# Output stores moved to ScalarE's queue, constants and copies spread over three engines: a fused attention and mixture-of-experts kernel on Trainium2

## The chip, the cores and the metric

The kernel runs on one core of one Trainium2 chip. In it TensorE does the matrix products, VectorE, ScalarE and GpSimd the elementwise work, and SyncE issues transfers, as do GpSimd and, after the change, ScalarE. The granted clock is the share of TensorE's full clock that the trace shows. The metric is the device time of one launch in microseconds (us), the median of several runs; the outputs are compared with the reference each time. A run is labelled slow when it is more than 1.5 per cent above the fastest of its kernel; ratios use the other runs only.

## The reference, cut to what matters

Eight batches, eight heads, 576 tokens, 64 values a head. Each batch goes through attention with a window of 32 tokens to either side, then the whole batch goes to one of eight experts, chosen by the mean of its attention output.

```python
scores = scale * np.matmul(q, k.transpose(0, 1, 3, 2))     # |i - j| <= 32 only
attn = np.exp(scores); attn = attn / attn.sum(-1)
x = attn @ v                                               # (8, 576, 512)
logits = x.mean(axis=1) @ w_gate                           # pick one expert e per batch
out[b] = gate * (np.maximum(x[b] @ w1[e], 0.0) @ w2[e])    # w1 512x1024, w2 1024x512
```

The expert isn't known before the batch's attention is done, so its 4 MB of weights are asked for at that moment, from an address read out of a register.

## The kernel before

A small planner in the kernel's Python holds a list of operations, each with an engine, an estimated duration, what it depends on and which buffers it takes and frees. It simulates them and emits a fixed order for each engine. What it believes of a transfer therefore decides the order in which instructions stand. The parts that matter here (cuts are marked `# ...`):

```python
buffers("osb", [P, DM], FP32, 3)          # output tiles of 128 tokens, three of them
# ...
end = at[op.eng] = t + op.dur
over = end + self.LAT[op.eng]
if op.land:                               # transfers: one after another at 370 GB/s
    dma_at = max(dma_at, end + 1.3) + op.land / (self.DMA_GBS * 1e3)
    over = dma_at + 0.7                   # from here on the planner takes it as landed
# ...
def loadw(op):                            # expert weights, fp32 to fp16, by GpSimd's DMA queue
    nc.gpsimd.dma_start(w1s, moe_w1[ds(ereg, 1)][0].rearrange("(p dt) f -> p dt f", p=P))
# ...                                     # loadw2 the same for w2
def evac(op, i=i):                        # ScalarE: PSUM -> osb, times the gate
    osb = op.got["osb"][0]
    nc.scalar.activation(osb[:, 0:w], bank_of.pop(f"2{b}{i}")[:, 0:w], ACTF.Copy, ...)
plan.add("ACT", 0.69 if i < 4 else 0.43, f"V{b}{i}", evac, ..., takes=[("osb", 1)])

def store(op, i=i):                       # SyncE: osb -> DRAM, five tiles a batch
    if i < 4:
        nc.sync.dma_start(out[b, 128 * i : 128 * i + 128, :], osb); return
    for c in range(2):
        nc.sync.dma_start(out[b, 512:576, 256 * c : 256 * c + 256], osb[64 * c : 64 * c + 64, 0:256])
plan.add("SP", 0.6 if i < 4 else 1.2, f"O{b}{i}", store, deps=[f"V{b}{i}"], frees=[(f"V{b}{i}", "osb")], ...)
```

An eviction is ScalarE's copy of a finished result out of PSUM, the memory that TensorE writes. A batch has five evictions (four of 128 tokens and a tail of 64) and three `osb` tiles. The fourth eviction needs the tile of the first, so it needs the first store landed; the fifth needs the second.

The softmax here doesn't subtract the row's maximum and nothing guards it: scores larger than these inputs give would overflow.

## Time and profile before

| | before |
|---|---|
| median of 3 runs | 276.94 us (276.49 to 279.07) |
| span of the profiled run | 277.2 us |
| TensorE busy | 227.2 us |
| mean period from batch to batch (six of them) | 28.6 us |
| landing of a store, median of 33 away from weights / of 15 beside them | 2.2 / 10.5 us (5.7 to 17.2) |

TensorE is the busiest engine, and it still stands or runs at half clock for long enough that the run is much longer than its work. From the page of the kernel before: the first line of the busy times, and the shares of the chain of work that ended last (followed back from the last instruction).

```profile
PE 227.2 (82%) x2432; PEld 174.5 (63%) x2432; DVE 160.0 (58%) x447; ACT 155.2 (56%) x329; POOL 72.3 (26%) x86
...
PE 53%; DVE 21%; DMA 14%; ACT 6%; issue 4%; POOLq 0%; ACTq 0%; DVEq 0%; SPq 0%
```

### The profile page before, as it was taken

The page shows a single profiled execution, that of the slowest core. Times are in us where ns is not written, and L with a number is a line of the kernel's source. Part 1 is how long each engine was busy: PE and PEld are TensorE (multiplying, and loading weights), DVE is VectorE, ACT ScalarE, POOL GpSimd, SP SyncE. Part 2 cuts the span into 40 slices and gives each one's busy share as a digit, 9 for nine tenths or more (in the row PEclk, how much of TensorE's full clock was granted, in tenths as well). Part 3 has the DMA queues.
Part 4 walks back from the last instruction along what each step waited for, and adds up shares of the span by engine and source line. Part 5 has one row for each costly group of instructions (what it writes and reads, how often), then busy time and mean ns, then how long its engine had stood idle before and what let it go on. Part 6 is the DMA issues. An engine that isn't in the chain of part 4 may idle for free.

```text
span 277.2 us, 6188 instructions
## 1 busy us (share of the span) xinstructions
PE 227.2 (82%) x2432; PEld 174.5 (63%) x2432; DVE 160.0 (58%) x447; ACT 155.2 (56%) x329; POOL 72.3 (26%) x86
## 2 busy tenths in 40 slices
PE   0374786799989986978977669999999999966993
PEld 0263674597689755767566646698599679633651
DVE  7999999716684659477589615375479454100000
ACT  1055256276688645469248545299559848412542
POOL 8639006001504602270604106130154000100000
PEclk9998588589999999599999959999999999985698
DMA  7979905900999799899934999249986971396113
GB/s 254 285 239 384 359 21 82 217 7 2 197 263 386 167 232 348 282 223 247 379 118 71 223 325 314 95 108 231 314 275 182 203 195 58 38 225 156 57 60 113
DMA packets 26877, 55.00 MB, mean 198 GB/s; under 512 B 2304, under 2 KB 12512, under 8 KB 24800
## 3 DMA queue, kind: packets, MB, share of 16 engines
q1 hardware_dynamic: 24544, 37.83, 38.8%
q0 software_dynamic: 2304, 16.78, 31.8%
q8 instruction: 19, 0.31, 0.4%
q14 instruction: 10, 0.08, 0.1%
HBM read 61.94 MB, written 9.44 MB: 257 GB/s over the span
## 4 chain that ended last, share of the span: by engine, by line
PE 53%; DVE 21%; DMA 14%; ACT 6%; issue 4%; POOLq 0%; ACTq 0%; DVEq 0%; SPq 0%
PE bank L652 25%; PE bank L688 13%; DMA out_dram<-osb 11%; DVE E L476 4%; PE bank L502 4%; DMA w<-in_moe_w_dram 3%; PE bank L538 3%; DVE xs L524 3%; DVE kT L295 2%; DVE qT L295 2%; PE bank L429 2%; PE bank L381 2%; ACT E L457 2%; ACT hT L670 2%; ACT osb L714 1%
## 5 line engine op out<-in xcount | busy, mean ns | idle before, releaser
L652 PE MATMUL bank<-xT,w 128*128 128x288 f16 x512 | 85.9, 314 | 12.9 <-ACT osb L714 7.4
L652 PEld LDWEIGHTS <-w 128*128 128x128 f16 x512 | 64.4, 149 | 21.1 <-issue 13.8
L670 ACT ACTIVATE hT<-bank 128x288 f16<-128x288 f32 x128 | 51.5, 416 | 33.5 <-PE bank L652 31.3
L688 PE MATMUL bank<-w,hT 128*128 128x512 f16 x256 | 61.4, 379 | 0.0
L320 POOL CAST qkb<-raw 128x1152 bf16<-128x1152 f32 x30 | 35.7, 1206 | 63.8 <-DMA raw<-in_q_dram 49.3
L457 ACT ACTIVATE E<-bank 128x512 f16<-128x512 f32 x72 | 40.0, 606 | 4.7 <-PE bank L429 4.5
L297 ACT COPY xT<-bank 128x512 f16<-128x512 f16 (+1 forms) x40 | 21.6, 543 | 34.2 <-PE bank L538 33.6
L502 PE MATMUL bank<-vaug,E 128*128 128x65 f16 x576 | 29.8, 203 | 10.3 <-DVE E L471 2.5
L714 ACT ACTIVATE osb<-bank,gwb 128x512 f32<-128x512 f32 (+1 forms) x40 | 25.0, 645 | 23.6 <-PE bank L688 13.5
L381 PE MATMUL bank<-id_bf,qkb 128*128 128x128 bf16 x288 | 26.1, 236 | 14.2 <-POOL qkb L320 9.5
L688 PEld LDWEIGHTS <-hT 128*128 128x128 f16 x256 | 23.3, 98 | 21.3
L502 PEld LDWEIGHTS <-E 128*128 128x128 f16 x576 | 26.1, 104 | 15.7 <-issue 6.8
L524 DVE TENSOR_TENSOR xs<-bank,linv 128x256 f16<-128x256 f32 (+1 forms) x80 | 33.8, 423 | 2.8
L297 ACT COPY qT<-bank 64x640 bf16<-64x640 bf16 (+1 forms) x32 | 23.5, 745 | 20.4 <-DVE qT L295 19.0
L476 DVE TENSOR_TENSOR E<-E,mask 128x384 f16<-128x384 f16 (+1 forms) x64 | 28.5, 468 | 10.7 <-ACT E L457 10.5
L522 DVE RECIPROCAL linv<-bank 128x4 f32<-128x4 f32 (+1 forms) x80 | 13.9, 173 | 34.2 <-PE bank L502 34.0
L381 PEld LDWEIGHTS <-qkb 128*128 128x128 bf16 x288 | 21.0, 107 | 18.1 <-POOL qkb L320 9.5
L622 POOL DMA_DIRECT2D w<-in_moe_w_dram x8 | 4.8, 597 | 91.1 <-DVE gw L615 66.0
L429 PE MATMUL bank<-qT,kT 128*128 128x128 bf16 x288 | 25.1, 230 | 3.5 <-DVE kT L295 1.7
L295 DVE COPY kT<-bank 128x640 bf16<-128x640 bf16 (+1 forms) x32 | 24.1, 758 | 3.2 <-PE bank L381 3.1
L429 PEld LDWEIGHTS <-kT 128*128 128x128 bf16 x288 | 20.6, 103 | 8.2 <-issue 3.6
L295 DVE COPY qT<-bank 64x640 bf16<-64x640 bf16 (+1 forms) x32 | 24.1, 757 | 2.1 <-PE bank L381 2.0
(57 smaller groups left out, 157.3 us busy)
## 6 DMA issues: line engine op xcount, KB each, us to landing
w<-in_moe_w_dram POOLq DMA_DIRECT2D x16, 1024.0 KB, 10.4
raw<-in_q_dram SPq DMA_DIRECT2D x16, 576.0 KB, 14.2
raw<-in_k_dram SPq DMA_DIRECT2D x16, 576.0 KB, 15.5
out_dram<-osb SPq DMA_DIRECT2D x32, 256.0 KB, 2.7
out_dram<-osb SPq DMA_DIRECT2D x16, 64.0 KB, 2.2
vraw<-in_v_dram SPq DMA_DIRECT2D x8, 0.2 KB, 14.9
vraw<-in_v_dram SPq DMA_DIRECT2D x8, 8.0 KB, 13.2
vraw<-in_v_dram SPq DMA_DIRECT2D x1, 24.0 KB, 6.8
```

The lines of the kernel that those rows point to most:

```text
L295: nc.vector.tensor_copy(dst, src)
L297: nc.scalar.copy(dst, src)
L320: (nc.vector if op.eng == "DVE" else nc.gpsimd).tensor_copy(t, raw[(b, quad, name)].rearrange("p h j d -> p j h d"))
L381: nc.tensor.transpose(pv[:, j - j0, :], raw[(b, quad, name)][:, j], id_bf)
L429: nc.tensor.matmul(dst, qkT[(b, a, "k")][:, k0 : k0 + P], qkT[(b, a, "q")][:, :, k0 : k0 + 64], start=(m == 0), stop=True, skip_group_chec ...
L457: nc.scalar.activation(dst, src, ACTF.Exp, bias=0.0, scale=0.125)
L476: nc.vector.tensor_tensor(ev, ev, mask[:, 1:2].unsqueeze(1).broadcast_to([P, 2, m, 64]), ALU.mult)
L502: nc.tensor.matmul(bank[:, hp * 65 : hp * 65 + 65], E_of[b][:, h, c0 : c0 + P], va_of[b][:, late, slot, 0:65], start=(hp == 0 and n == 0), ...
L524: nc.vector.tensor_tensor(xv[:, par], hv[:, :, 0:64], linv.to_broadcast([n, 4, 64]), ALU.mult)
L652: nc.tensor.matmul(bank[:, 0:288], w_of[b][0].rearrange("p t (c n) -> p t n c", c=P)[:, dt, ft], xT_of[b][:, dt, 288 * c : 288 * c + 288], ...
L670: nc.scalar.activation(h_of[(b, ft)][:, 288 * c : 288 * c + 288], bank_of.pop(gn)[:, 0:288], ACTF.Relu,)
L688: nc.tensor.matmul(bank, h_of[(b, ft)][:, 128 * i : 128 * i + 128], w2s[:, ft, :], start=(ft == 0), stop=(ft == NFT - 1),)
```

## The change

Its intent: stores should no longer stand behind loads in SyncE's queue, nor loads behind stores; constants should be ready sooner; copies should go to whichever of VectorE and ScalarE is idle. The core of the diff (cut to what counts; one hunk per part):

```diff
@@ the planner
+            if op.land and op.eng == "ACT":
+                dma_at = max(dma_at, end + 1.3) + op.land / (self.DMA_GBS * 1e3)
+                over = end + 2.6
-            if op.land:
+            elif op.land:
@@ stores
-                    nc.sync.dma_start(out[b, 128 * i : 128 * i + 128, :], osb)
+                    nc.scalar.dma_start(out[b, 128 * i : 128 * i + 128, :], osb)
-                for c in range(2):
-                    nc.sync.dma_start(out[b, 512:576, 256 * c : 256 * c + 256], osb[64 * c : 64 * c + 64, 0:256])
-            plan.add("SP", 0.6 if i < 4 else 1.2, f"O{b}{i}", store, ...
+                nc.scalar.dma_start(out[b, 512:576].rearrange("s (c d) -> c s d", c=2), osb[:, 0:256])
+            plan.add("ACT", 0.5, f"O{b}{i}", store, ...
@@ constants: qT memsets GpSimd -> VectorE, gaps of E VectorE -> ScalarE, first k casts VectorE -> GpSimd
-        nc.gpsimd.memset(qTs[n][64:128, 0], 0.0)
+        nc.vector.memset(qTs[n][64:128, 0], 0.0)
-        nc.vector.memset(Es[n].rearrange("p h (i c) -> p (h i) c", c=P)[:, :, 64:P], 0.0)
+        nc.scalar.copy(Es[n].rearrange("p h (i c) -> p (h i) c", c=P)[:, :, 64:P], zero...)
@@ copies of q, k and x^T
-                        plan.add("ACT" if h2 == 1 else "DVE", 0.74 if first else 0.6,
+                        plan.add(BOTH, 0.74 if first else 0.6,
-            plan.add("ACT", 0.58 if i < 4 else 0.25, "C" + xn, xcopy,
+            plan.add(BOTH, {"DVE": 0.44, "ACT": 0.6} if i < 4 else {"DVE": 0.28, "ACT": 0.4}, "C" + xn, xcopy,
@@ tails
-    xss = buffers("xs", [P, DM], FP16, 7)
+    buffers("xs", [P, DM], FP16, 6)
+    xls = buffers("xl", [P, DM], FP16, 2)
```

The first hunk moves no data, but it tells the planner that a store on ScalarE's queue has always landed 2.6 us after its issue.

More of the change, by code (lines that the diff above doesn't have):

```diff
@@ L134, in finish @@
             op.emit(op)
-            end = at[op.eng] = t + op.dur
+            end = at[op.eng] = t + (op.dur[op.eng] if isinstance(op.dur, dict) else op.dur)
             over = end + self.LAT[op.eng]
-            if op.land:
+            if op.land and op.eng == "ACT":
+                dma_at = max(dma_at, end + 1.3) + op.land / (self.DMA_GBS * 1e3)
+                over = end + 2.6
+            elif op.land:
                 dma_at = max(dma_at, end + 1.3) + op.land / (self.DMA_GBS * 1e3)
@@ L216, with zeros @@
     onec = sb.tile([P, 1], FP16, name="onec")
-    onet = sb.tile([P, 1], FP16, name="onet")
+    zero = sb.tile([P, 64], FP16, name="zero")
     wg_sb = sb.tile([P, NDT, NE], FP32, name="wg_sb")
+    def zeros(op):
+        nc.gpsimd.memset(zero, 0.0)
+        for t in vraws:
+            nc.gpsimd.memset(t[0:32, 0], 0.0)
+            nc.gpsimd.memset(t[32:64, NVS], 0.0)
+            nc.gpsimd.memset(t[64:P, NVS], 0.0)
     def constants_a(op):
@@ L229, in constants_a, with constants_q, constants_b @@
         nc.vector.tensor_single_scalar(id_bf, rel[:, 0:P], 0.0, ALU.is_equal)
+    def constants_q(op, n):
+        nc.vector.memset(qTs[n][64:128, 0], 0.0)
+        nc.vector.memset(qTs[n][0:64, 1], 0.0)
+    def constants_b(op):
         for t in kTs:
@@ L232, in constants_a @@
             nc.vector.memset(t[:, KPAD + 2 * S :], 0.0)
-    def constants_q(op, n):
-        nc.gpsimd.memset(qTs[n][64:128, 0], 0.0)
-        nc.gpsimd.memset(qTs[n][0:64, 1], 0.0)
-    def constants_b(op):
         nc.vector.tensor_single_scalar(low, rel[:, 0:64], 0.0, ALU.is_le)
@@ L244, in constants_b @@
             )
-        nc.vector.tensor_single_scalar(id_f16, rel[:, 0:P], 0.0, ALU.is_equal)
         nc.vector.memset(mask[0:W, 0], 0.0)
@@ L249, in constants_c, with gaps @@
     def constants_c(op):
+        nc.vector.tensor_single_scalar(id_f16, rel[:, 0:P], 0.0, ALU.is_equal)
         nc.vector.memset(onec, 1.0)
-        nc.vector.memset(onet[0:64], 1.0)
-        nc.vector.memset(onet[64:128], 0.0)
-        for t in xss:
+        for t in xls:
             nc.vector.memset(t[64:128], 0.0)
-        for t in vraws:
-            nc.gpsimd.memset(t[0:32, 0], 0.0)
-            nc.gpsimd.memset(t[32:64, NVS], 0.0)
-            nc.gpsimd.memset(t[64:P, NVS], 0.0)
-    def constants_d(op, n):
-        nc.vector.memset(vaugs[n][:, :, :, D : D + 1], 1.0)
-        nc.vector.memset(
-            Es[n].rearrange("p h (i c) -> p (h i) c", c=P)[:, :, 64:P], 0.0
-        )
-    plan.add("DVE", 1.9, "ca", constants_a, prio=-10)
-    plan.add("DVE", 2.5, "cb", constants_b, deps=["ca"], prio=30)
-    plan.add("DVE", 1.0, "cc", constants_c, prio=-20)
-    plan.add("DVE", 1.8, "cd0", lambda op: constants_d(op, 0), deps=["ca"], prio=-5)
-    for n in range(3):
-        plan.add("SW", 1.2, f"cq{n}", lambda op, n=n: constants_q(op, n), prio=-5 + 100 * n)
-    plan.add("DVE", 1.8, "cd1", lambda op: constants_d(op, 1), deps=["ca"], prio=700)
+        for t in vaugs:
+            nc.vector.memset(t[:, :, :, D : D + 1], 1.0)
+    def gaps(op, n):
+        nc.scalar.copy(
+            Es[n].rearrange("p h (i c) -> p (h i) c", c=P)[:, :, 64:P],
+            zero.unsqueeze(1).broadcast_to([P, H * NQB, 64]),
+        )
+    plan.add("SW", 1.2, "zero", zeros, prio=-30)
+    plan.add("DVE", 3.3, "ca", constants_a, prio=-20)
+    plan.add("DVE", 0.8, "cq0", lambda op: constants_q(op, 0), prio=-19)
+    plan.add("DVE", 1.2, "cb", constants_b, deps=["ca"], prio=-18)
+    plan.add("DVE", 1.4, "cc", constants_c, deps=["ca"], prio=-17)
+    plan.add("DVE", 0.8, "cq1", lambda op: constants_q(op, 1), deps=["cc"], prio=-16)
+    plan.add("DVE", 0.8, "cq2", lambda op: constants_q(op, 2), deps=["cq1"], prio=-15)
+    plan.add("ACT", 5.0, "cd0", lambda op: gaps(op, 0), deps=["zero"], prio=-10)
+    plan.add("ACT", 3.6, "cd1", lambda op: gaps(op, 1), deps=["cd0"], prio=-9)
     def emit_wg(op):
@@ L319, in cast @@
                     t = op.got["qkb"][0]
-                    (nc.vector if op.eng == "DVE" else nc.gpsimd).tensor_copy(
+                    nc.gpsimd.tensor_copy(
                         t, raw[(b, quad, name)].rearrange("p h j d -> p j h d")
@@ L323, in cast @@
                     raw[(b, quad, name)] = t
-                plan.add("DVE" if b == 0 and name == "k" else "SW", 1.2, f"c{name}{b}{quad}", cast,
+                plan.add("SW", 1.2, f"c{name}{b}{quad}", cast,
                          deps=[f"ld{name}{b}{quad}"], takes=[("qkb", 1)],
@@ L345, in add_batch @@
         plan.add("SP", 1.2, f"ldv{b}", loadv, takes=[("vraw", 1)], land=1.5e6, prio=base + 2,
-                 deps=[f"W2{b - 2}_"] if b > 1 else ["cc"])
+                 deps=[f"W2{b - 2}_"] if b > 1 else ["zero"])
         for part in range(4):
@@ L361, in add_batch @@
             plan.add("SW" if part < 2 else "DVE", 1.25 if part < 2 else 1.3, f"vc{b}{part}", vcast,
-                     deps=[f"ldv{b}"] + (["cd0"] if b == 0 else ["cd1"] if b == 1 else [])
+                     deps=[f"ldv{b}"] + (["cc"] if b == 0 else [])
                      + ([f"vc{b}0"] if part == 1 else [f"vc{b}1"] if part > 1 else []),
@@ L402, in tcopy @@
                             copy(op, dst.rearrange("p (c j) -> p c j", j=J)[:, :, j0:j1], pv)
-                        plan.add("ACT" if h2 == 1 else "DVE", 0.74 if first else 0.6,
+                        plan.add(BOTH, 0.74 if first else 0.6,
                                  f"C{tn}{h2}", tcopy,
                                  deps=[tn] + ([f"C{tn}0"] if h2 == 1 else [])
-                                 + ([f"cq{n}" for n in range(3)] if b == 0 and h2 < 2 else []),
+                                 + ([f"cq{b}"] if b < 3 and h2 < 2 else []),
                                  frees=[(tn, "psA")] if h2 else [],
@@ L440, in add_batch @@
                      + [f"CT{b}{a}k{p}2" for p in range(2) for a in quads]
+                     + (["cb"] if b == 0 else [])
                      + ([f"S{b}000_"] if n else [])
@@ L509, in add_batch @@
                 last = i == NQT - 1 and par == 1
-                plan.add("PE", 0.25, an, av, deps=masked[i] + (["cc", "cb", "cd0"] if b == 0 else ["cd1"] if b == 1 else []),
+                plan.add("PE", 0.25, an, av, deps=masked[i] + (["cc", f"cd{b}"] if b < 2 else []),
                          takes=[("psA", 1)],
@@ L516, in norm @@
                     if par == 0:
-                        xs_of[(b, i)] = op.got["xs"][0]
+                        xs_of[(b, i)] = op.got["xs" if i < 4 else "xl"][0]
                     xs = xs_of[(b, i)]
@@ L528, in add_batch @@
                          deps=[an] + ([f"NA{b}{i}0"] if par else []), frees=[(an, "psA")],
-                         takes=[("xs", 1)] if par == 0 else [], prio=base + 520 + 80 * i)
+                         takes=[("xs" if i < 4 else "xl", 1)] if par == 0 else [], prio=base + 520 + 80 * i)
             xn = f"R{b}{i}"
@@ L550, in xcopy @@
                 copy(op, xT_of[b][:, :, 128 * i : 128 * i + n], pv[:, :, 0:n])
-            plan.add("ACT", 0.58 if i < 4 else 0.25, "C" + xn, xcopy,
+            plan.add(BOTH, {"DVE": 0.44, "ACT": 0.6} if i < 4 else {"DVE": 0.28, "ACT": 0.4},
+                     "C" + xn, xcopy,
                      deps=[xn] + ([f"CR{b}0"] if i else []),
@@ L564, in pool @@
                         xs_of[(b, i)].rearrange("t (p n) -> t n p", p=P)[:, dt],
-                        onet if i == NQT - 1 else onec,
+                        onec,
                         start=(dt == 0 and i == 0), stop=(i == NQT - 1),
@@ L570, in add_batch @@
                  takes=[("psA", 1)],
-                 frees=[(f"NA{b}{i}0", "xs") for i in range(NQT)], prio=base + 930)
+                 frees=[(f"NA{b}{i}0", "xs" if i < 4 else "xl") for i in range(NQT)], prio=base + 930)
         def poolc(op):
@@ L724, in store @@
                 if i < 4:
-                    nc.sync.dma_start(out[b, 128 * i : 128 * i + 128, :], osb)
+                    nc.scalar.dma_start(out[b, 128 * i : 128 * i + 128, :], osb)
                     return
-                for c in range(2):
-                    nc.sync.dma_start(
-                        out[b, 512:576, 256 * c : 256 * c + 256],
-                        osb[64 * c : 64 * c + 64, 0:256],
-                    )
-            plan.add("SP", 0.6 if i < 4 else 1.2, f"O{b}{i}", store, deps=[f"V{b}{i}"],
+                nc.scalar.dma_start(
+                    out[b, 512:576].rearrange("s (c d) -> c s d", c=2), osb[:, 0:256]
+                )
+            plan.add("ACT", 0.5, f"O{b}{i}", store, deps=[f"V{b}{i}"],
                      frees=[(f"V{b}{i}", "osb")], land=262e3 if i < 4 else 140e3, prio=mo - 5000)
```

## The prediction

> **What bounds the kernel now.** I read in this order: the page's slices, the chain of waits for marks to cut the run at, the wait lists of all engines and of the DMA queue, then the timeline where it looked odd.
>
> The slices first. Each digit is a tenth of busy time in a fortieth of the span (6.9 us).
>
> ```profile
> PE   0374786799989986978977669999999999966993
> ...
> PEclk9998588589999999599999959999999999985698
> DMA  7979905900999799899934999249986971396113
> ```
>
> TensorE works at 9 over long stretches, so it is the engine to feed, but it starts late, has two troughs (around 100 to 125 and 140 to 170 us) and a weak end. Its granted clock falls to half in five places. DMA is nearly full except around 36 to 68 us.
>
> For marks I take the pooling matmuls (L562, 20 per batch): batch b's attention is done there and its expert can be chosen. From the chain of waits:
>
> ```profile
> 64.23 0.64 PE bank L562 x20
> ...
> 68.81 10.00 DMA out_dram<-osb
> ...
> 88.83 0.64 PE bank L562 x20
> ...
> 236.09 0.64 PE bank L562 x20
> ```
>
> The timeline has batch 0's pooling end at 39.6. So the run is 39.6 us to the first mark, 25.3 to the second (64.9), six periods of together 171.8 (28.6 each) to the last (236.7), and 40.5 from there to 277.2. A period holds one attention and one MoE. Full-clock pieces of the chain price it: 64 first-layer matmuls at 0.99 us per 8 are 7.9 us, 32 of the second layer at 1.73 per 8 are 6.9, its 16 tail ones 1.0, transposes and scores 36 each at 0.45 per 8 are 4.0, 72 of attention-times-v at 0.72 per 24 are 2.2, 20 transposes of x at some 0.22 per 4 are 1.1, pooling and gate 0.9. Sum 24.0. The first two periods took 24.6 and 24.2; the other four average 30.7, so 27 us are lost between the marks.
>
> The chain's second line says where: a store took 10 us, and evictions waited for it. Waits of all engines (waiter, releaser: us in total, times, longest), then of the DMA queue:
>
> ```profile
> ACT osb L714 <- DMA out_dram<-osb: 9.0, 3, 4.8
> PE bank L652 <- ACT osb L714: 7.4, 3, 4.6
> ```
> ```profile
> SPq L725 <- ACT osb L714: 108.2, 21, 33.3
> ```
>
> SyncE, in order, stood 108 us at stores whose data wasn't there, with loads queued behind; and stores stand behind loads:
>
> ```profile
> 27.91 7.63 SPq L344 DMA_DIRECT2D vraw<-in_v_dram  x1
> 68.81 0.37 SPq L725 DMA_DIRECT2D out_dram<-osb  x1
> 69.28 0.37 SPq L308 DMA_DIRECT2D raw<-in_q_dram  x1
> ...
> 121.28 17.86 SPq L344 DMA_DIRECT2D vraw<-in_v_dram  x1
> 139.25 0.37 SPq L725 DMA_DIRECT2D out_dram<-osb  x1
> ```
>
> Loads of batch 3 went out at 69.28, the moment the first store had gone; a v load's issue held the queue 17.86 us and the next store came only then.
>
> The start: GpSimd casts q only after its memsets, k's cast sits behind VectorE's constants, and VectorE clears the second E buffer in the middle of batch 0's attention.
>
> ```profile
> 8.35 2.23 POOL L320 CAST qkb<-raw 128x1152 bf16<-128x1152 f32 x2
> ...
> 11.51 1.35 DVE L320 CAST qkb<-raw 128x1152 bf16<-128x1152 f32 x1
> ...
> 20.76 1.98 DVE L262 MEMSET E<- 128x2304 uint32 x1 [0.41 <-issue]
> ...
> 23.94 1.61 DVE L360 COPY vaug<-vaug 64x2304 f16<-64x2304 f16 x1
> ```
>
> The end: the last batch's weights arrive at 248.0; then ScalarE has six ReLUs ahead of two evictions that hold two of three PSUM banks until 257.8, so each step costs 1.6 us instead of 0.5, at half clock.
>
> ```profile
> 248.00 1.16 PE L652 MATMUL bank<-xT,w 128*128 128x288 f16 x4 [1.90 <-DMA w<-in_moe_w_dram]
> 249.66 1.12 PE L652 MATMUL bank<-xT,w 128*128 128x288 f16 x4 [0.50 <-ACT hT L670]
> ```
>
> **What the Trainium skill says.** "DMA: Bandwidth & Descriptors", section "Queues, rings and completion order": SP and ACT each have a row of rings on the same 16 engines, and an engine goes round robin between rows by packet. The trace agrees with the second half: while GpSimd's weight stream runs, its packets (8 KB, 0.62 us) alternate with SyncE's (2 KB, 0.1 us). A store, 8 packets per engine, issued at 68.81 just after the weights at 68.27, landed at 78.81; those of 240.81 and 242.45, with no loads about, took 10.2 and 11.5; away from weights it is 2.0. So a row of its own frees a store from the loads, not from the weights.
> Same page, "Why a DMA increments its semaphore by 16 and not by 1": the count of engines divides the slowest dimension of both sides. The merged tail store has a DRAM side of 2x64x256, so perhaps 2 engines; no run yet shows it.
> "TensorE: Matmul & The Clock Gate", "What's actually happening": the clock is halved after idleness. Agrees: after 4.6 us of idle at 157 to 162, granted 0.50 from 159.7 to 166.
> "ScalarE: Activation LUTs", "What ACT_TABLE_LOAD costs": 186 ns plus 0.833 per element. The 512-element exponential fits (613 against 606 in the row).
>
> **The change part by part.**
> Constants. GpSimd's six qT memsets (6 x 1.05 us) go to VectorE as 32-bit words (576 words each, from the E memset's 0.86 ns per word some 0.6); casts of k go to GpSimd; VectorE loses 2 x 1.98 of E memsets, 2.7 of casts and 5 of 7 xs memsets (1.4). ScalarE gets two E clears of 4,608 elements, estimated at 4.0 us each, in its idle first 12 us. Loads landed at 4.5, 5.9, 8.1 and 9.5, so four casts of 1.2 end near 5.8, 7.2, 9.3 and 10.7; before, the last ended at 15.8. VectorE and ScalarE then finish the copies near 16 (before 20), the exponentials near 21 (24.3), and attention-times-v starts near 21 to 22 instead of being whole at 28. Batch 0's mark: 39.6 less 7.3 = 32.3.
> Second stretch: first weights, first MoE at half clock as now; 25.3.
> Copies. ScalarE had 32 q copies and 40 of x^T; now 44 q/k and 17 x^T: 23 x^T copies fewer at some 0.54 are -12.5 us, 12 q/k copies more at 0.75 are +9: about even in sum, but spread to whichever of the two engines is idle.
> Stores. 40 issues of about 0.4 us on ScalarE: +2 us a batch, of which its 19.4 us a batch has room. Removed: the waits above (PE lost 8.5 us directly in five waits for evictions, with 3 more of slow clock), the 17.9 us holds, the late loads. The order listing shows every period now alike: transposes, scores and second layer, then attention and first layer. With free stores I put a period at 24.0/0.955 = 25.2 (the share TensorE reached in its good stretch, 170 to 240), 25.7 with ScalarE's issues: 154.
> Tail: evictions now stand before the ReLUs. With free stores: weights land 11.7 us after the mark, the first layer takes 11 (slow clock at first), second 7.9, store and end 5.4: 36.
> Sum, free stores: 32.3 + 25.3 + 154 + 36 = 248.
> What gives it back: weights are asked for 3.4 to 3.9 us after each mark, exactly when the five evictions and stores come. Three osb buffers: the fourth eviction needs store 1, issued near 5.5, landed near 15.7; the fifth needs store 2, which lands when the weights do, near 19. ScalarE is in order: five exponentials and all ReLUs stand behind. Behind the fifth: 0.5 + 4 x 0.6 + 16 x 0.42 + 2 x 0.59 + 0.4 = 11.1, so a period of 30.1, +4.4 on each of six, and a tail of 41: in full 32.3 + 25.3 + 181 + 41 + 2 for the two-engine store = 282. The order was laid out for a 2.6 us landing everywhere. I can't tell how much an own ring eases it; I take a bit over half the cost: 248 + 19 = 267.
>
> **Rivals.** (1) Free stores: a separate ring gets its turns quickly; 248. For: the 2.7 us median landing. Against: the 10 us cases had no loads in front. (2) The osb wait moves onto ScalarE and stalls every period: 282, up to 290 if TensorE also falls to half clock in each. Also the program shares eight DMA semaphores in turn among loads and stores, so some stores must wait for a load, on ScalarE. (3) DMA bound: its busy share of 0.70 of 277 us is 24.4 us a batch, as much as TensorE's work; loads that start earlier could push weights back; about 258. (4) ScalarE bound by issues in the second-layer phase (13.9 us of work against TensorE's 12.2): up to 1.7 a period, 258.
>
> **Range and chances.** Between 248 and 282 lies everything I can argue; the prologue's 7 us is safest. 267, 8 in 10 from 247 to 287. Faster 0.55, same 0.22, slower 0.23.
>
> **What would show it.** Batch 0's pooling end near 32; loads no longer behind stores; marks 25 to 26 apart (free) or 30 (stalled); in the wait list, the eviction's wait for the output DMA: near 0 or 30 and more us; store landings beside weights, 2 to 3 or 10; TensorE's half clock gone or in every period; the last store 2 or 5 us. I am wrong in kind if marks are 25 apart with 10 us landings, or if the start gains nothing.

## The result, and the profile after

| | before | after |
|---|---|---|
| median of four runs each, same session | 277.98 us | 304.14 us (302.67 to 304.65) |
| ratio of the fast runs | | 1.094, 95% interval 1.086 to 1.101 |

A ratio here and below is the mean time of one kernel's fast runs over that of the other's of the same rounds, so it isn't quite the ratio of the medians. The change costs 9 per cent. The prediction had 267 with a range up to 287.

First the page of the changed kernel: busy times, slices of 7.6 us, the shares of the chain, and the stores' line of the DMA issues (count, size, median us from issue to landing).

```profile
PE 231.4 (76%) x2432; PEld 177.3 (59%) x2432; DVE 168.9 (56%) x453; ACT 163.5 (54%) x320; POOL 68.4 (23%) x83
...
PE   1475878995899649995699729993599929975990
...
PEclk9996975999599958997599958997599977995798
...
PE 49%; DMA 31%; DVE 8%; ACT 5%; issue 4%; ACTq 0%
...
out_dram<-osb ACTq DMA_DIRECT2D x32, 256.0 KB, 10.5
```

TensorE's row now has a regular beat: full, a hole, half clock, full again, once a batch. DMA has gone from 14 to 31 per cent of the chain, and the wait list says whose transfer it is (waiter, releaser: us in all, times, longest):

```profile
ACT osb L726 <- DMA out_dram<-osb: 53.5, 13, 6.7
...
PE bank L513 <- ACT E L468: 30.2, 9, 5.6
```

ScalarE's evictions wait 53.5 us for stores, 9.0 before. TensorE's attention-times-v (L513) waits 30 us for exponentials that stand behind those evictions on ScalarE.

One period in the chain of waits of the changed kernel (start, length, what). The mark is the end of the pooling matmuls, L574:

```profile
124.57 0.64 PE bank L574 x20
...
131.39 0.63 ACT osb L726
132.05 13.84 DMA out_dram<-osb
...
146.34 0.60 ACT E L468
...
158.71 0.63 PE bank L574 x20
```

The same stretch in ScalarE's timeline: first and second store issued, then the fourth and the fifth eviction with the wait before each in brackets, then the exponential behind it.

```profile
129.49 0.34 ACTq L737 DMA_DIRECT2D out_dram<-osb  x1
...
138.89 0.69 ACT L726 ACTIVATE osb<-bank,gwb 128x512 f32<-128x512 f32 x1 [3.52 <-DMA out_dram<-osb]
...
145.97 0.47 ACT L726 ACTIVATE osb<-bank,gwb 128x256 f32<-128x256 f32 x1 [5.91 <-DMA out_dram<-osb]
146.34 0.59 ACT L468 ACTIVATE E<-bank 128x512 f16<-128x512 f32 x1
```

Store 1, issued at 129.49, frees the fourth eviction at 138.89; store 2, issued at 132.05, frees the fifth at 145.97. Now set beside this when the batch's two weight loads landed: W1 at 138.65 and W2 at 145.72. Each store lands with a weight load. The records of the single packets say why. A weight load is 128 packets of 8 KB, eight on each of the 16 DMA engines; a store is 128 packets of 2 KB, eight per engine too. (The page's 10.5 us for a store is a median of nine: the profile gives no landing for the other 23 of the 32.) Counted from the trace in stretches of 2 us (packets begun, and mean duration of one):

```
from    weights (GpSimd's queue)    stores (ScalarE's queue)
132     44 at 0.63 us               40 at 0.10 us
134     43 at 0.62                  45 at 0.10
136     47 at 0.62                  42 at 0.09
138     41 at 0.62                  42 at 0.08
140     39 at 0.68                  38 at 0.08
142     17 at 0.83                  58 at 0.08
144      1                          179 at 0.08
```

As long as weights flow, one store packet goes for one weight packet, although it has a quarter of the bytes. A store of eight packets per engine costs eight weight packets of 0.62 us, and the second store of a batch has to wait until the first is through. When the weights end, 179 packets go in 2 us. SyncE's loads take turns too, from 136 us on (12, 46, 34 and 81 packets in the four stretches). And a landing waits for its last engine: W2 ends with 16 packets of 4 bytes, of which fifteen begin from 143.27 to 143.89 and the last at 145.36, so about 1.5 us of that landing are one late engine's.

Finally the same period cut in four by the windows view (stretch: length, busy time and count of each engine, granted clock, DMA share, GB/s): up to the second store's issue, its flight, the stretch after it, and the rest.

```profile
125.04:132.05 7.01, 7.01 (x76) 4.49 (x75) 6.23 (x15) 4.88 (x10) 2.89 (x5) 1.00 0.26 30
132.05:145.97 13.92, 8.79 (x83) 5.77 (x81) 8.08 (x13) 3.97 (x7) 5.29 (x5) 0.80 1.02 261
145.97:151.00 5.03, 4.09 (x36) 3.09 (x36) 3.04 (x9) 3.60 (x9) 0.00 (x0) 0.55 1.07 382
151.00:159.20 8.20, 8.20 (x123) 8.12 (x119) 4.59 (x17) 6.18 (x15) 0.00 (x0) 1.00 0.44 136
```

TensorE is full in the first and the last stretch. In the second it has 8.8 us of work for 13.9, and after it has idled, the third has a granted clock of 0.55.

The sum by marks, in us (the ends of the pooling):

| stretch | before | after |
|---|---|---|
| start to the first mark | 39.6 | 33.7 |
| first to second | 25.3 | 23.6 |
| six periods | 171.8 | 205.2 |
| last mark to the end | 40.5 | 40.2 |

The start got 5.9 us shorter and the second stretch 1.7; the six periods took 33.4 more, 34.2 each instead of 28.6.

### The profile page after: what moved, and what is told of

It is laid out like the page before. It is cut to its first block, busy times and chain, and to the rows that moved or that the text cites. A ratio compares the mean times of both kernels' runs of the same rounds, so it can differ in the third digit from the quotient of the medians.

```text
span 302.7 us, 6131 instructions
## 1 busy us (share of the span) xinstructions
PE 231.4 (76%) x2432; PEld 177.3 (59%) x2432; DVE 168.9 (56%) x453; ACT 163.5 (54%) x320; POOL 68.4 (23%) x83
## 4 chain that ended last, share of the span: by engine, by line
PE 49%; DMA 31%; DVE 8%; ACT 5%; issue 4%; ACTq 0%
DMA out_dram<-osb 28%; PE bank L664 25%; PE bank L700 9%; PE bank L513 5%; PE bank L391 4%; PE bank L549 3%; DMA w<-in_moe_w_dram 3%; ACT E L468 2%; ACT osb L726 2%; PE bank L574 1%; DVE E L487 1%; ACT kT L307 1%; DVE qT L305 1%; PE bank L439 1%; PE bank L596 1%
## 5 line engine op out<-in xcount | busy, mean ns | idle before, releaser
L664 PE MATMUL bank<-xT,w 128*128 128x288 f16 x512 | 90.3, 333 | 12.6 <-ACT osb L726 7.3
L664 PEld LDWEIGHTS <-w 128*128 128x128 f16 x512 | 66.5, 151 | 23.6 <-issue 9.0
L513 PE MATMUL bank<-vaug,E 128*128 128x65 f16 x576 | 33.9, 210 | 39.4 <-ACT E L468 30.2
L700 PE MATMUL bank<-w,hT 128*128 128x512 f16 x256 | 63.6, 379 | 0.0
L726 ACT ACTIVATE osb<-bank,gwb 128x512 f32<-128x512 f32 (+1 forms) x40 | 25.7, 642 | 64.6 <-DMA out_dram<-osb 53.5
L487 DVE TENSOR_TENSOR E<-E,mask 128x384 f16<-128x384 f16 (+1 forms) x64 | 34.6, 550 | 38.9 <-ACT E L468 38.9
L513 PEld LDWEIGHTS <-E 128*128 128x128 f16 x576 | 29.2, 109 | 43.6 <-issue 32.5
L305 DVE COPY qT<-bank 64x512 bf16<-64x512 bf16 (+1 forms) x46 | 35.3, 774 | 2.1 <-PE bank L391 0.6
L391 PE MATMUL bank<-id_bf,qkb 128*128 128x128 bf16 x288 | 25.4, 234 | 10.2 <-POOL qkb L330 7.6
L535 DVE TENSOR_TENSOR xs<-bank,linv 128x256 f16<-128x256 f32 x64 | 27.1, 424 | 2.2
L439 PEld LDWEIGHTS <-kT 128*128 128x128 bf16 x288 | 20.3, 103 | 10.2 <-issue 4.7
L307 ACT COPY kT<-bank 128x512 bf16<-128x512 bf16 (+1 forms) x26 | 18.4, 736 | 9.7 <-PE bank L391 9.6
L305 DVE COPY xT<-bank 128x512 f16<-128x512 f16 (+1 forms) x23 | 8.8, 384 | 25.9 <-PE bank L549 25.8
L365 POOL CAST vaug<-vraw 128x1152 f16<-128x1152 f32 (+1 forms) x16 | 18.9, 1236 | 6.8 <-DMA vraw<-in_v_dram 6.8
L533 DVE RECIPROCAL linv<-bank 128x4 f32<-128x4 f32 (+1 forms) x80 | 13.9, 174 | 8.6 <-PE bank L513 8.1
## 6 DMA issues: line engine op xcount, KB each, us to landing
w<-in_moe_w_dram POOLq DMA_DIRECT2D x16, 1024.0 KB, 11.9
out_dram<-osb ACTq DMA_DIRECT2D x32, 256.0 KB, 10.5
vraw<-in_v_dram SPq DMA_DIRECT2D x8, 0.2 KB, 11.2
```

Of the source, the lines that this page charges most:

```text
L305: nc.vector.tensor_copy(dst, src)
L391: nc.tensor.transpose(pv[:, j - j0, :], raw[(b, quad, name)][:, j], id_bf)
L439: nc.tensor.matmul(dst, qkT[(b, a, "k")][:, k0 : k0 + P], qkT[(b, a, "q")][:, :, k0 : k0 + 64], start=(m == 0), stop=True, skip_group_chec ...
L487: nc.vector.tensor_tensor(ev, ev, mask[:, 1:2].unsqueeze(1).broadcast_to([P, 2, m, 64]), ALU.mult)
L513: nc.tensor.matmul(bank[:, hp * 65 : hp * 65 + 65], E_of[b][:, h, c0 : c0 + P], va_of[b][:, late, slot, 0:65], start=(hp == 0 and n == 0), ...
L535: nc.vector.tensor_tensor(xv[:, par], hv[:, :, 0:64], linv.to_broadcast([n, 4, 64]), ALU.mult)
```

## The experiments

Twelve kernels ran. The changed kernel itself ran only in the session of the result: a difference to it crosses sessions, a ratio to before doesn't. "Order kept" means that the list of instructions of the engines named was compared with that of the kernel it starts from and is the same. The first theory, *turns*: a store lands only as fast as weight packets let it, the planner's order counts on 2.6 us, and three buffers turn that into stands of ScalarE and then of TensorE.

**e1_osb6: six output buffers, order kept on every engine.** The planner still plans with three; the tiles are used in turn.

```diff
-    buffers("osb", [P, DM], FP32, 3)
+    osbs = buffers("osb", [P, DM], FP32, 6); plan.resource("osb", osbs[0:3])
-                osb = op.got["osb"][0]
+                osb = osbs[(NQT * b + i) % 6]
```

> The changed kernel with six output buffers instead of three, used in turn; every engine keeps its order of instructions. Theory (turns): in the changed kernel each 2 KB store packet waits for one 8 KB weight packet of 0.62 us, so a store (8 packets per DMA engine) lands only with a weight load (8 packets per engine as well), and the fourth and fifth evictions of a batch need the first two stores. Six buffers take that need away without making a store faster: evictions wait for stores under 10 us in all (53.5 before), stores beside weights still land 9 to 14 us after issue, marks come 25 to 27 us apart instead of 34.2, total 245 to 262. Rival A (ScalarE loses its time to issuing and to DMA semaphores shared in turn by loads and stores): it goes on waiting, now at the issues; total above 285. Rival B (the new order is bad for TensorE whatever the stores do): 285 to 300.

Measured: 265.59 us, ratio to before 0.957 (0.941 to 0.972), so 38.6 us less than the changed kernel from the buffers alone. The wait of evictions for stores has gone from the list, while the stores' median landing is still 10.5 us. Rivals A and B are out as the whole cause; the average period, 28.2 us, is above the 25 to 27 expected. The total is 3.6 above the range, and the chain of this run shows where: one period of 36 us among others of 25 to 29.

```profile
85.61 23.07 DMA vraw<-in_v_dram
...
108.76 0.54 ACTq L739
109.34 0.60 ACT E L468
```

ScalarE stood from 98.2 (the end of the exponential before) to 108.76 at the issue of a tail store (L739), which has its data; it was let go when a v load landed at 108.68. The program's 90 hardware transfers use eight DMA semaphores in turn, and this store is the eighth transfer after that load's last part. So a piece of rival A is real, once in this run; e14_lane tests it.

**e6_wsplit: weight loads in four parts, so that a packet is 2 KB.** Three buffers, order kept on all engines but GpSimd.

```diff
-            nc.gpsimd.dma_start(w1s, moe_w1[ds(ereg, 1)][0].rearrange("(p dt) f -> p dt f", p=P))
+            w1d = moe_w1[ds(ereg, 1)][0].rearrange("(p dt) f -> p dt f", p=P)
+            for dt in range(NDT):
+                nc.gpsimd.dma_start(w1s[:, dt], w1d[:, dt])
```

(w2 likewise, two rows of `ft` at a time.)

> The changed kernel with each weight load cut into four, so that a packet is 2 KB and not 8; three output buffers, same order on TensorE, VectorE, ScalarE and SyncE; GpSimd issues 8 loads a batch in place of 2 (3.5 us more of its time). Theory (turns, packet for packet): a store packet now waits for a weight packet of some 0.16 us, so a store of 8 packets lands in 3 to 5 us even beside weights, the eviction's wait falls from 53.5 to under 15, the period from 34.2 to 25 to 28, total 248 to 268. Rival (the engines share by bytes, or memory itself is the limit): stores still take 9 to 14, total 295 to 310. Possible miss: the weights land later because GpSimd's issues and smaller packets are slower; then marks are 28 to 31 apart with short stores.

Measured: 277.77 us, ratio to before 1.010 (0.995 to 1.025): 26 less than the changed kernel, with the same bytes. The eviction's wait fell from 53.5 to 17.2 and the stores' landing to 6.9. So the size of the packets matters, at the same bytes; but 17.2 isn't under 15, 6.9 isn't the 3 to 5 expected, and the time is 10 above the range. Where both streams flow, from 122 to 126 us of this run, 257 weight packets stand beside 128 of the stores, so it is no longer one for one. Why it is about two to one with small packets no run here shows. The "possible miss" came in part: marks are some 30 us apart.

**e2_spq: stores issued by SyncE in the changed order.** Order kept on TensorE, VectorE and GpSimd; ScalarE loses its 40 issues.

```diff
-                    nc.scalar.dma_start(out[b, 128 * i : 128 * i + 128, :], osb)
+                    nc.sync.dma_start(out[b, 128 * i : 128 * i + 128, :], osb)
```

(the tail store likewise.)

> The changed kernel with the stores issued by SyncE instead of ScalarE, one store for the tail, and every other engine's order as it is. Theory (turns): SyncE's ring takes turns with the weights just as ScalarE's did, so stores of 8 packets still need 8 weight packets, and loads issued before them stand in front in the same ring: stores land as late or later, and the loads of later batches wait behind the stores; total 300 to 330. Rival A (ScalarE's own issuing of 40 stores at about 0.35 us, or its waits at the issue, are the cost): 14 us or more are won, total below 290.

Measured: 325.77 us, ratio to before 1.184 (1.169 to 1.199), 21.6 us slower than the changed kernel. SyncE's timeline in this run, two lines of it:

```profile
142.53 4.95 SPq L737 DMA_DIRECT2D out_dram<-osb  x1
...
151.33 10.47 SPq L354 DMA_DIRECT2D vraw<-in_v_dram  x1
```

A store's issue is itself held up, and the part of v's load that follows holds the queue for 10 us; the next store goes out at 161.9. Evictions wait 78.8 us. So ScalarE's queue was the better one for this order, and taking the 40 issues off ScalarE doesn't win the loss back. What they cost by themselves this run can't show, since it also puts stores and loads in one queue again; in another order the queue's worth turns round (e5).

**e4_stores: the stores' part alone, on the kernel before.** The two hunks "the planner" and "stores" of the diff, nothing else.

> The kernel before with the stores' part of the change alone: stores on ScalarE, planned as landing 2.6 us after the issue, the two tail stores merged. Constants, copies and tail buffers as before. Theory (turns, with an order that counts on 2.6 us): the eviction's wait for stores appears here in full (40 us and more), periods 33 to 35, total 303 to 318, the start 6 us later than in the changed kernel. Rival (the other parts, constants or copies on two engines, cause the loss): 262 to 280.

Measured: 302.70 us, ratio 1.101 (1.087 to 1.116). Evictions wait 48.7 us for stores, the first mark is at 40.0, the six periods are 32.9 each. This part alone loses as much as the whole change. Total and periods are just under the expected ranges; why its periods are 1.3 us shorter than the changed kernel's wasn't tested.

**e3_rest: everything but the stores' part.** Those two hunks undone in the changed kernel.

> The changed kernel with the stores' part undone: stores back on SyncE, planned with the queue's backlog, two tail stores; constants, copies and tail buffers as changed. Theory (the stores' part alone made the loss): no loss here, the first mark near 33 instead of 39.6, six periods like before's; total 264 to 274 against 277. Rival (constants and copies cost too, or lose what they win at the start as the DMA backlog holds the loads): 277 to 285.

Measured: 266.80 us median of four runs, 262.25 to 267.34, beside 282.52 for the kernel before in that session. Three of the four are labelled slow, since one run was 1.7 per cent faster, so there is no ratio with an interval; the one fast run, 262.25, stands beside two of 274.95 and 278.29. The first mark is at 34.5 (39.6 before). Constants, copies and tail buffers win some 14 us (fast runs) to 16 (medians); the loss isn't theirs. In its wait list the evictions wait 3.6 us for stores, 9.0 before.

**e5_backlog: one number of the planner.** Stores stay on ScalarE with three buffers, but the planner takes them to land after all transfers planned before.

```diff
-            if op.land and op.eng == "ACT":
-                dma_at = max(dma_at, end + 1.3) + op.land / (self.DMA_GBS * 1e3)
-                over = end + 2.6
-            elif op.land:
+            if op.land:
```

> The changed kernel with one number of the planner changed: it takes a ScalarE store to land after all transfers planned before it, as before, not 2.6 us after its issue. Stores stay on ScalarE with three buffers; the planner now puts the later evictions of a batch behind exponentials and ReLUs. Theory (not the queue but an order that counts on free buffers makes the loss): evictions wait under 20 us in all for stores (53.5), total 268 to 288, stores beside weights as slow as ever (9 to 14 us). Rival (any order with stores on ScalarE stalls): 295 and more.

Measured: 277.74 us, ratio to before 1.008 (0.987 to 1.028). Evictions wait 8.7 us for stores. What the planner believed of the queue, and the order that came of that belief, made the 26 us between this kernel and the changed one. But that isn't the whole of the stores' part: in the same session e3, with the stores on SyncE and the same belief, took 266.80 (its one fast run 262.25), 11 to 15 us less than this. With six buffers in both, 8.6 us remain (e11 and e13 below, 261.63 and 270.25). So in the cautious order the move to ScalarE's queue loses. The two also differ in the merged tail store and in the order that the planner makes of it; which of these costs the 11 us wasn't tested.

**e7_wsplit_osb6: six buffers and weights in four parts.** The edits of e1 and e6 together.

> Both cures on the changed kernel: six output buffers and weights in four loads each of 2 KB packets; same order on TensorE, VectorE and ScalarE. With six buffers alone it took 265.6, with 2 KB packets alone 277.8. Theory: once no eviction waits for a store, quicker stores win nothing, and the slower weights (last quarter lands 15 to 16 us after the first is asked for, 14 to 16 in one piece) and starved v loads cost something: 262 to 272, the one 11 us stand of ScalarE at a store's issue (it waited for a v load) perhaps gone. Rival (stores' speed itself matters further): 250 to 258.

Measured: 276.50 us, ratio to before 0.998 (0.981 to 1.014): 11 more than with six buffers alone and above the range; both readings missed. GpSimd's timelines, first of e7 (mark at 149.4), then of e1 (mark at 121.7):

```profile
155.66 2.44 POOL L645 DMA_DIRECT2D w<-in_moe_w_dram  x4
...
158.26 2.36 POOL L365 CAST vaug<-vraw 128x1152 f16<-128x1152 f32 x2
```

```profile
126.88 2.35 POOL L365 CAST vaug<-vraw 128x1152 f16<-128x1152 f32 x2
```

GpSimd issues eight loads instead of two, so v's casts start 8.9 us after the mark instead of 5.2. In e7 the chain goes through them: cast, two copies of v on VectorE, masks, then attention-times-v. That is the 3.5 us of issuing named in the expectation of e6, on the path. The 3.7 us of delay are of the size of the 3.3 by which e7's periods (30.0 on average) exceed e1's usual ones (26.7 without the long one). That is a reading of the chain; no run undid it.

**e12_before_osb6: the kernel before with six buffers.** The edit of e1, order kept.

> The kernel before with six output buffers in turn and nothing else; every engine keeps its order. Its profile had ScalarE waiting 9.0 us in three for stores and TensorE 7.4 us behind that. Theory: those waits go, some 5 to 9 us: 268 to 273 beside 277. Rival (SyncE's holds at v loads and stores stay the bound, since the order is the same): within 1%.

Measured: 267.20 us, ratio 0.964 (0.947 to 0.980). By the ratio the wait for buffers was worth 10 us in the kernel before as well, without any queue moved; a little more than the 5 to 9 expected.

**e14_lane: e1 with one store moved.** Order kept but for this one issue.

```diff
-                nc.scalar.dma_start(
+                (nc.sync if b == 1 else nc.scalar).dma_start(
                     out[b, 512:576].rearrange("s (c d) -> c s d", c=2), osb[:, 0:256]
                 )
```

> The changed kernel with six output buffers, and one store (the second batch's tail) issued by SyncE instead of ScalarE; all else in the same order. In the run with six buffers ScalarE stood 11 us at that store's issue until a v load of 23 us had landed: the eight DMA semaphores go round among loads and stores, and this store is the eighth transfer after the v load. Theory: moved, the load takes the turn after v and ScalarE doesn't stand: the third mark to the fourth is 26 to 28 us instead of 36, total 254 to 258. Rival (the stand was only a shadow of loads that arrive late): the same period waits elsewhere, total 262 to 266.

Measured: 257.19 us median, the two fast runs 253.6 and 253.7, ratio to before 0.918 (0.902 to 0.934). The period of 36 us is now 25.7. The stand at the issue was real time, and it came from semaphores shared in turn between loads and stores. The move also shifts the semaphores of the transfers around it by a turn: the trace has this store on the semaphore of a k load, no longer on that of the v load. This version beats both kernels. Two periods of it by the windows view, to be set beside the four lines of the changed kernel above:

```profile
111.10:138.50 27.40, 25.16 (x307) 20.12 (x305) 21.71 (x53) 18.74 (x39) 8.20 (x9) 1.00 1.04 302
138.50:165.50 27.00, 25.46 (x309) 20.30 (x307) 21.59 (x53) 18.68 (x39) 8.20 (x9) 1.00 0.95 262
```

A period's work on TensorE now takes 25 us, at full clock, in a period of 27.

**e11_rest_osb6: e3 with six buffers.**

> The changed kernel without its stores' part (stores on SyncE in the old order, 266.8) and with six output buffers. Theory: the two gains add: 266.8 less the 3.6 per cent that six buffers gave the kernel before is 257; range 254 to 262. Rival (SyncE's stands at stores then bind): 263 to 267.

Measured: 261.63 us, ratio 0.946 (0.934 to 0.958), in the range but at its slow end. The two gains don't add: 15 us by the ratio, against 10 for the buffers alone and about 14 for the rest alone. The rest had already taken away most of what evictions waited for stores (3.6 us were left of 9.0). In the same session e14 has a ratio of 0.918: moving the stores wins some 4 us (medians) to 8 (fast runs) over this kernel, but only with six buffers and without the one stand (e1, with the stand, has 0.957).

**e13_backlog_osb6: e5 with six buffers.**

> Stores on ScalarE in the order of the planner that counts the DMA backlog (277.7 with three buffers), with six buffers. Theory: this order spreads the evictions already, so buffers win less than the 38 us they win in the changed order: 264 to 274. Rival: evictions still waited in that order and the stands go: 254 to 262.

Measured: 270.25 us, ratio 0.976 (0.963 to 0.990). In the cautious order six buffers win 7.5 us, in the changed order 38.6. With buffers enough, the trusting order of the changed kernel is the better of the two (265.6, and 257.2 without the one stand).

**e16_thin: the changed kernel with only an eighth of W2 loaded.** The rest is zeros, so the output is wrong; order kept on all engines but GpSimd.

```diff
-                w2s, moe_w2[ds(w_of[b][2], 1)][0].rearrange("(p ft) d -> p ft d", p=P)
+                w2s[:, 0:1], moe_w2[ds(w_of[b][2], 1)][0].rearrange("(p ft) d -> p ft d", p=P)[:, 0:1]
```

> The changed kernel, three buffers, same order on TensorE, VectorE, ScalarE and SyncE; of the second layer's weights only an eighth is loaded (the rest is zeros, set once by GpSimd), so the output is wrong on purpose. Theory (a store packet waits for a weight packet, one for one): the stream by the side of the stores has some 9 large packets per DMA engine instead of 16. The first store still takes its 8 turns and lands about when the first weights do, 9 us after issue; the second finds the ring free and lands 2 to 4 us later instead of 7; the fifth eviction comes 4 to 6 us sooner in each period: 28 to 31 us between marks instead of 34.2, total 268 to 285 (the zeros may cost some us at the start). Rival (the stores are slow by themselves on ScalarE's ring, or for the loads of q, k and v): the period stays above 33.

Measured: 281.49 us, ratio to before 1.030 (1.000 to 1.059), with a start of 39.6 us (the zeros) and periods of 29.3 instead of 34.2. ScalarE's timeline, fourth and fifth eviction:

```profile
139.47 0.69 ACT L729 ACTIVATE osb<-bank,gwb 128x512 f32<-128x512 f32 x1 [4.32 <-DMA out_dram<-osb]
...
141.66 0.47 ACT L729 ACTIVATE osb<-bank,gwb 128x256 f32<-128x256 f32 x1 [1.02 <-DMA out_dram<-osb]
```

The first store lands as late as ever, with W1; the second is through 2.2 us after it instead of 7.1. The stream of weights is what slows a store; that its packets' size matters, and not its bytes alone, is e6's part.

## Why the prediction was wrong

**The mechanism was foreseen, the weight given to it was not.** The prediction's second rival said that the wait for output buffers would move onto ScalarE and stall every period. The trace shows its steps in each of the six periods (12 of the 13 waits; one is at the end). The failed step is the sentence "I can't tell how much an own ring eases it; I take a bit over half the cost". It eases nothing beside weights: there stores take 9 to 14 us from ScalarE's queue, and took 10.5 (median) from SyncE's. The prediction had the evidence in hand (stores of 10.2 and 11.5 us with no loads about) and hedged against it.

**The stalled case itself was 21 us too small.** It summed to 282. The parts: start 33.7 against 32.3, second stretch 23.6 against 25.3, tail 40.2 against 43, and six periods 205.2 against 181. A period was to be 19 us to the fifth eviction and 11.1 from there to the next mark (its terms add to 11.2). Over the six periods the fifth eviction starts 18.6 to 20.8 us after the mark, 19.5 on average, so that term was right; the period shown above, with 20.8, is a long one. The mis-sized term is what stands behind: 13.4 to 15.7 us, 14.7 on average. The prediction counted ScalarE's work there, at full clock (it allowed up to 290 in all for a half clock). But the chain leaves ScalarE after an exponential or two and runs on TensorE to the mark: TensorE is busy for 13.75 of the 14.7 us, at a mean granted clock of 0.81. At full clock the 14.7 would be some 11.9, an estimate from these two numbers. In three of the periods the first 16 first-layer matmuls after the stand take 3.84 us in the chain, in e14 1.99 to 2.18. Together 4 us a period.

Smaller slips: the windows view gives TensorE 68.96 of 70 us busy from 170 to 240, a share of 0.985, not 0.955; before, the weights were asked for 2.7 to 4.0 us after a mark, not 3.4 to 3.9; the half clock begins at 159.4, not 159.7. None of them decides.

**The start** was right in kind and near in size: 5.9 us won against 7.3, and e3, without the stores' part, has its first mark at 34.5.

**The copies** ("about even in sum") weren't tested by themselves; in e3 they are part of the 14 us won.

**The stores' issues on ScalarE** take 0.34 us each, as expected, but what they cost was not isolated: e2 takes them away and is slower for another reason, and the 11 us between e3 and e5 are open.

**The shared semaphores** were named as an aside. In the changed kernel they are hidden behind the stands; with six buffers they cost 11 us in one place (e1, e14).

**The merged tail store**: 2 us were put down for it. At the end of the changed kernel its 128 packets begin over 3.2 us, from 297.5 to 300.7, while those of the two tail stores of the kernel before begin within 1.0, from 274.5 to 275.5. So the size is right; no run undid it alone. "DMA: Bandwidth & Descriptors", section "Why a DMA increments its semaphore by 16 and not by 1", lets one expect that this store uses two engines, and that each engine in use ends with a write to the semaphore. The trace agrees: after its data ScalarE's queue has two packets of 4 bytes, where a store of 256 KB has 16.

**Rival 1, free stores,** was worked out as 248 with periods of 25.7. When the buffers and the one semaphore are out of the way, e14 shows a span of 251.9 and periods of 26.4. The sum was sound; the premise needed six buffers.

**Rival 3, bound by DMA,** is out as far as the changed kernel goes: in e14 the same bytes flow in 252 us, at a DMA share near 1.0 in its periods. It may well be the next bound. **Rival 4**, bound by ScalarE's issues, is out too: in e14, with 39 of the 40 issues on ScalarE, it works 18.7 us of a period of 27.

## What to carry to other kernels

A queue of its own takes a store out from behind the loads, not out from beside a stream of large packets: count packets per engine on both sides. Here one store packet went for each weight packet of 8 KB, and about one for two of 2 KB. When a planner or your own ordering assumes a landing time, check it where the DMA is busiest, and give the buffer that waits for the landing enough copies to cover the real one; here three 2 KB-per-partition tiles more were worth 38.6 us in the changed order and 10 in the old one. A stand costs more than its length where TensorE loses its clock over it: here 0.81 on average for the rest of the period. And a queue is worth only what the order makes of it: the move of the stores lost 9 to 15 us in the cautious order (e3 and e5, e11 and e13) and won 4 to 8 in the trusting one, once buffers and the one semaphore were out of the way (e11, e14).

## What the Trainium skill lacked or had wrong

- "DMA: Bandwidth & Descriptors", section "Queues, rings and completion order", says that an engine goes round robin between rows and drains a whole packet, typically 9 to 17 descriptors, before it switches. The turns are there, but the unit is smaller in this trace: if a store's eight pieces per engine went in one turn, it would land after one weight packet. It needs eight: 42 store pieces of 2 KB begin in the 2 us in which 47 weight pieces of 8 KB do, and the eviction that needs the first store starts at 138.89, when the weight load has landed at 138.65.
- The page gives no figure for a small transfer beside a large one: here 9 to 14 us for a 256 KB store instead of 2.0, whichever of the two queues it is issued from. With weight pieces of 2 KB the ratio was no longer even (257 to 128 in 4 us); no run here shows why.
- No page that was consulted speaks of a program that uses a few DMA semaphores in turn for all its loads and stores, so that a store with its data ready holds its engine until an unrelated load has landed: 11 us in one place here.
- "TensorE: Matmul & The Clock Gate", section "What's actually happening", puts the halving after an idle window of some 3.4 us. In the changed kernel the granted clock fell to 0.50 at about 140.3, after TensorE had been idle for 2.47 us by the trace; in the 3.4 us before it matmuls had still run for 0.9.
